# Who issues the output stores: ScalarE's queue or SyncE's, in a one-core attention and Fourier-mix kernel

## The chip, the cores and the metric

The kernel runs on one core of a Trainium2 chip. The metric is the time of one execution on the device, in microseconds (us). Eight executions of the kernel before gave a median of 308.81 us, from 307.64 to 309.92.

An engine of the core works through its own list of instructions in order: TensorE (PE) multiplies matrices, VectorE (DVE) and ScalarE (ACT) do element work, GpSimd (POOL) does some element work, and SyncE (SP) here issues transfers (DMAs) and nothing else. POOL and ACT issue DMAs too. A transfer is carried out by 16 shared DMA engines after its issue; the issuing engine goes on meanwhile. An instruction that waits holds up everything behind it on its own engine.

## The reference

Two stages, for 4 batches of 768 rows:

```python
# attention in chunks of 32 queries, each with 8 memory keys and its neighbourhood
scores = scale * np.matmul(q_c, k_full.transpose(0, 1, 3, 2))
a = softmax(scores)                      # per row
out[:, :, c_start:c_end] = np.matmul(a, v_full)
...
# x = out, heads joined: (4, 768, 512)
X = np.fft.fft(np.fft.fft(x, axis=1), axis=2)
u = x + np.real(X)
un = (u - mu) / np.sqrt(var + 1e-06)     # mean and variance of each row
ch = np.maximum(un @ w_ch1, 0.0) @ w_ch2 # 512 -> 2048 -> 512
return u + ch
```

## The kernel before, in words

**Stages.** Each batch b goes through three stages. *Attention* takes 4 pairs of heads per batch, 16 pairs n in all: POOL loads q and k (L287), SP loads v with seven DMAs of short rows (`e_load_v`, L290 to L306, into one of four tiles `va`), PE turns and multiplies, ACT takes the exponential, DVE divides (`e_norm`) into the batch's tile `xs[b]`. *Fourier*: DVE folds the rows, PE multiplies with sine and cosine tables (`ps`, L446, then `pm`, L588), DVE adds the result to the input. The upper three of a batch's six row tiles are wanted in mirrored order. For batches 1 to 3 that is done by three transfers: POOL writes the rows to DRAM (`x_rows`, L478), SP copies them there in reverse order (`x_back`, L482 and L483), POOL reads them again (`xr`, L487), and `e_sum_back` (DVE, L502 and L504) adds them to `pm`. Each DVE sum frees one of the two PSUM buffers that `pm` uses. After the sums come row statistics (L600, L601), `un` on ACT (L606) and, for batches 1 to 3, a transposing DMA on SP (`unT`, L618), which the text calls a flip. *MLP*: per half batch 16 groups of `ph` (L644) with a relu on ACT (L651), then three output tiles of 16 matmuls each (`pc`, L658). DVE makes each output tile `osb` (L664); there are three `osb` buffers.

**Outputs.** The six row tiles (0, 0 to 5) of batch 0 and tiles 0 to 2 of the later batches go straight to the output (`e_out`, L668). Tiles 3 to 5 of batches 1 to 3 lie mirrored and go in two hops: `e_out_rows` (L671) writes the tile to DRAM, and `e_out_back` (L678 and, for tile 3, L680) copies it in reverse order to the output. The MLP makes a batch's tiles in the order 0, 1, 2, 3, 4, 5 for batch 0 and 0, 3, 4, 5, 1, 2 for the others. In the text, "store (b, t)" is the transfer that takes tile t of batch b out of `osb`. In the kernel before ACT issues all 24 stores, and SP issues the second hops.

**Order.** Before anything is emitted, a planner (`Plan`, L37 to L137) runs through the tasks with guessed costs and fixes the order of every engine's list. At each step it takes, for each free engine, the first task in rank that is ready. A task is ready when its predecessors are done, and, for a task with `lag`, when they have been done for that long:

```python
if any(a["done"] is None
       or (a["end"] > now if a["engine"] == e else a["done"] > now - slack - t["lag"])
       for a in t["after"]):
```

A predecessor on the task's own engine is compared without the lag. `moved` is a guess of the transfer's time; transfers of one engine follow each other in the plan, and the task counts as done 1.4 us after that. `take` and `give` count buffers, `osb` among them. Loads of v (SP) keep their order; tasks marked `loose` may go past a load that isn't ready. The rank of a task is its place in the program, and the MLP's tasks come after all of attention and Fourier, so on SP a load of v, an `x_back` or a flip that is ready goes ahead of a second hop.

**Completion counters.** In the compiled program of the kernel before, the DMAs that SP and ACT issue take eight completion counters in turn, one common round for both engines, and a DMA waits until the previous DMA on its counter has landed, whichever engine issued that one and whatever it moved.

Of the kernel before, what the change touches and what calls it, by code (L numbers as in the profile page):

```python
# [36 lines left out]
class Plan:  # L37
# [6 lines left out]
    WARM = 14.0  # L44
    SLACK = 0.7
    FILL = 0.17
    LATER = 14.0
    filling, fill = None, None

    def __init__(self, slots):  # L50
# [3 lines left out]
    def add(self, engine, cost, emit, after=(), take=(), give=(), rank=None, moved=0.0,  # L54
            loose=False, late=0.0, filler=False, behind=None, push=False, lag=0.0):
        t = dict(engine=engine, cost=cost, emit=emit, after=[a for a in after if a is not None],
                 take=take, give=give, rank=len(self.tasks) if rank is None else rank,
                 moved=moved, done=None, at=None, no=len(self.tasks), loose=loose,
                 late=late, filler=filler, behind=behind, push=push, lag=lag)
        self.tasks.append(t)  # L60
        return t

    def order(self):
        now, idle, wire = 0.0, {}, {}
        waiting = {}
        for t in self.tasks:
            waiting.setdefault(t["engine"], []).append(t)
        for ts_ in waiting.values():
            ts_.sort(key=lambda t: (t["rank"], t["no"]))
        gives = []  # L70
        placed = []
        while any(waiting.values()):
            for tag in [g for g in gives if g[0] <= now]:
                gives.remove(tag)
                self.free[tag[1]] += 1
            moved = False
            for e, ts_ in waiting.items():
                if idle.get(e, 0.0) > now:
                    continue
                held = False  # L80
                for t in ts_:
                    slack = (self.SLACK if e == "PE" and now > self.FIRST and not t["filler"]
                             else 0.0)
                    if held and not t["loose"]:
                        continue
# [3 lines that stand above are left out]
                        held = held or (e == "SP" and not t["loose"])  # L89
                        continue  # L90
                    if t["behind"] is not None and t["behind"]["at"] is None:
                        continue
                    need = {}
                    for tag in t["take"]:
                        need[tag] = need.get(tag, 0) + 1
                    if any(self.free[tag] < m for tag, m in need.items()):
                        held = held or (e == "SP" and not t["loose"])
                        continue
                    for tag in t["take"]:
                        self.free[tag] -= 1  # L100
                    cost = t["cost"] * (2.0 if e == "PE" and now < self.WARM else 1.0)
                    idle[e] = t["end"] = now + cost
                    if t["moved"]:
                        wire[e] = max(wire.get(e, 0.0), now + cost) + t["moved"]
                        t["done"] = t["end"] = wire[e] + (2.8 if e == "POOL" else 1.4) + t["late"]
                        if t["push"] and wire.get("SP", 0.0) > now:
                            wire["SP"] += t["moved"]
                            for o in placed:
                                if o["engine"] == "SP" and o["done"] > now:
                                    o["done"] += t["moved"]  # L110
                                    o["end"] = o["done"]
                    else:
                        t["done"] = now + cost + self.LAG.get(e, 0.07)
                    for tag in t["give"]:
                        gives.append((t["done"], tag))
                    t["at"] = now
                    placed.append(t)
                    ts_.remove(t)
                    moved = True
                    break  # L120
                else:
                    if e == "PE" and self.filling and self.filling[0]["at"] is not None \
                            and self.filling[1]["at"] is None:
                        cost = self.FILL * (2.0 if now < self.WARM else 1.0)
                        idle[e] = now + cost
                        placed.append(dict(engine="PE", cost=cost, emit=self.fill, at=now,
                                           done=now + cost))
                        moved = True
            if not moved:
                times = ([v for v in idle.values() if v > now] + [g[0] for g in gives]  # L130
                         + [t["done"] + x for t in placed for x in (0.0, self.SLACK, self.LATER)
                            if t["done"] + x > now])
                assert times, [(t["engine"], t["no"], t["take"]) for ts_ in waiting.values()
                               for t in ts_[:2]]
                now = min(x for x in times if x > now)
        self.end = max(t["done"] for t in placed)
        return placed  # L137
# [3 lines left out]
def kernel(  # L141
# [11 lines left out]
    nc = tc.nc  # L153
    B, H, S, D = q.shape
    DM = out.shape[2]
    DFF = moe_w_ch1.shape[1]
    P = 128
# [35 lines left out]
    plan = Plan(dict(qs=NS, ks=NS, va=NV, kTb=NKT, qT=2, tr=1, sc=1, xa=1, e1=3,  # L193
                     xsb=3, fold=2, hl=1, up=4, dn=1, acc=2, mlp=2, un=6, unT=2, hT=1, osb=3))
# [470 lines left out]
                                       xs[b][:, st, :], ALU.mult, ALU.add)  # L665

    def e_out(b, st):
        nc.scalar.dma_start(out[b, ts(st, P), :], osb_of.pop((b, st)))  # L668

    def e_out_rows(b, st):  # L670
        nc.scalar.dma_start(od[b % 2, st - 3], osb_of.pop((b, st)))  # L671

    def e_out_back(b, st):
        t = st - 3
# [311 lines left out]
    def mlp(b, t_un, rs):  # L986
        for sh in range(2):
            relu = []
            c2 = None
            for ht in range(NHT):  # L990
                ph = add("PE", 0.65, lambda sh=sh, ht=ht: e_ch1(b, sh, ht),
                         mlp_prev + [t_un[slot(b, 3 * sh + i)] for i in range(3)] + t_w1,
                         take=(mtag(b, ht),), give=("unT",) if sh == 1 and ht == NHT - 1 else (),
                         rank=MLPS + len(plan.tasks), filler=True)
                relu.append(add("ACT", 0.5, lambda sh=sh, ht=ht: e_relu(b, sh, ht),
                                [ph, relu[-1] if relu else None],
                                take=("hT",) if ht == 0 else (), give=(mtag(b, ht),),
                                rank=RELU(len(plan.tasks))))
            for stl in range(3):
                st, end_b = slot(b, 3 * sh + stl), 3 * sh + stl == NST - 1  # L1000
                for part in range(4):
                    end = part == 3
                    c2 = add("PE", 0.88, lambda sh=sh, stl=stl, part=part: e_ch2(b, sh, stl, part),
                             [relu[4 * part + 3], t_w2[part], c2], take=(mtag(b, stl),) if part == 0 else (),
                             give=("hT",) if stl == 2 and end else (),
                             rank=MLPS + len(plan.tasks), filler=True)
                os_ = add("DVE", 0.76, lambda sh=sh, stl=stl: e_osb(b, sh, stl), [c2, rs],
                          take=("osb",), 
                          give=(mtag(b, stl), "xsb") if end_b else (mtag(b, stl),),
                          rank=RELU(len(plan.tasks)))  # L1010
                mlp_prev[0] = c2
                if b and st > 2:
                    o1 = add("ACT", 0.1, lambda st=st: e_out_rows(b, st), [os_], give=("osb",),
                             moved=0.9, late=1.5, rank=RELU(len(plan.tasks)))
                    add("SP", 0.1, lambda st=st: e_out_back(b, st), [o1], moved=2.6, loose=True,
                        lag=plan.LATER if b < B - 1 else 0.0)
                    continue
                add("ACT", 0.1, lambda st=st: e_out(b, st), [os_], give=("osb",), moved=0.9,
                    rank=RELU(len(plan.tasks)))

    def RELU(i):
        return i - MLPS
# [44 lines left out]
```

## Time and profile before

| | us |
|---|---|
| median of 8 executions | 308.81 |
| the profiled execution's own time | 309.92 |
| its span, first to last instruction | 308.2 |
| PE busy | 283.0 (92% of the span) |
| DVE busy | 168.4 (55%) |
| ACT busy | 163.0 (53%) |
| POOL busy | 45.6 (15%) |
| store issued by ACT (L668), one | 0.34 |
| first hop issued by ACT (L671), one | 0.33 |
| 256 KB second hop issued by SP (L678), one | 0.57 |
| mean granted PE clock | 0.982 of full |

In a timeline a row gives the start, the length, the engine and the line; SPq and ACTq are those engines' DMA issues, which do not count as busy. In the 40 equal slices of the page (7.7 us each) a digit is the busy share in tenths, or the granted clock in tenths of full speed. A row of the windows view gives, for a stretch, the busy time of PE, PEld (weight loads), DVE, ACT and POOL, then the granted clock, the share of the DMA engines and the GB/s.

### The profile page before, as it was taken

To read this page: it belongs to the slowest core of one execution; us is meant where nothing else is said; L and a number is where in the kernel's file an instruction comes from. 1 tells how busy PE (TensorE), PEld (TensorE's weight loads), DVE (VectorE), ACT (ScalarE), POOL (GpSimd) and SP (SyncE) were. 2 spreads that over 40 slices of the span, in tenths; PEclk is the share of its full clock that TensorE was granted. 3 is DMA by queue.
4 is the path that set the end of the run, shared out by engine and by line. 5 is a ranking of instruction groups with operands and counts; after the bars stand their busy time and mean duration, and the time that the engine had idled before them with its cause. 6 is when DMAs were issued, how large, how long until landed. Compare 5 with 4: busy or idle time off the path is not lost.

```text
span 308.2 us, 7397 instructions
## 1 busy us (share of the span) xinstructions
PE 283.0 (92%) x3086; PEld 176.5 (57%) x3086; DVE 168.4 (55%) x368; ACT 163.0 (53%) x291; POOL 45.6 (15%) x84
## 2 busy tenths in 40 slices
PE   1399998999999991799999999999999999999994
PEld 0357677866656770465578555765554554554641
DVE  7868896874298760837986949946801101002001
ACT  6656356688684762385875832572471360630710
POOL 8806421131031002111001021000010000000000
PEclk9999999999999997599999999999999999999999
DMA  6989999998487498946493225921630423103404
GB/s 117 195 174 170 208 203 197 198 200 161 88 186 152 118 140 196 176 88 178 114 169 103 53 53 188 195 97 46 130 66 34 105 34 95 43 0 89 84 34 102
DMA packets 98689, 38.36 MB, mean 124 GB/s; under 512 B 85728, under 2 KB 93920, under 8 KB 98656
## 3 DMA queue, kind: packets, MB, share of 16 engines
q1 hardware_dynamic: 84320, 16.33, 32.4%
q0 software_dynamic: 10592, 15.21, 25.2%
q10 hardware_dynamic: 3744, 6.36, 5.9%
q8 instruction: 24, 0.39, 0.5%
q14 instruction: 9, 0.07, 0.1%
HBM read 37.36 MB, written 13.37 MB: 165 GB/s over the span
## 4 chain that ended last, share of the span: by engine, by line
PE 85%; DMA 7%; POOL 2%; DVE 2%; issue 1%; SPq 1%; ACT 1%; POOLq 0%; DVEq 0%
PE pc L658 27%; PE ph L644 27%; PE xa L376 7%; PE ps L446 5%; PE idle L713 4%; PE pm L588 4%; PE ps L577 4%; PE sc L352 2%; DMA x_back<-x_rows 2%; DMA qs<-in_q_dram 2%; PE trk L314 2%; PE trq L314 2%; DMA xr<-x_back 2%; PE xo L376 1%; DVE st L600 1%
## 5 line engine op out<-in xcount | busy, mean ns | idle before, releaser
L644 PE MATMUL ph<-unT,w_sb 128*128 128x384 f16 x512 | 89.9, 329 | 0.7 <-ACT hT L651 0.6
L651 ACT ACTIVATE hT<-ph 128x384 f16<-128x384 f32 x128 | 61.0, 491 | 51.2 <-PE ph L644 49.6
L658 PE MATMUL pc<-w_sb,hT 128*128 128x512 f16 x384 | 87.5, 379 | 0.0
L644 PEld LDWEIGHTS <-w_sb 128*128 128x128 f16 x512 | 48.6, 98 | 33.9 <-issue 2.6
L664 DVE SCALAR_TENSOR_TENSOR osb<-pc,rstd,xsb 128x512 f32<-128x512 f32 x24 | 18.0, 750 | 77.1 <-PE pc L658 77.0
L658 PEld LDWEIGHTS <-hT 128*128 128x128 f16 x384 | 36.2, 98 | 41.2 <-issue 0.2
L360 ACT ACTIVATE e<-sc,mbias 128x384 f32<-128x384 f32 x64 | 33.7, 580 | 14.2 <-PE sc L352 13.5
L606 ACT ACTIVATE un<-xsb,mu_s 128x512 f16<-128x512 f32 x24 | 17.1, 718 | 23.2 <-DVE mu_s L601 23.2
L376 PE MATMUL xa<-va,e 128*64 128x65 f32 x672 | 25.7, 226 | 0.0
L376 PEld LDWEIGHTS xa<-va,e 128*64 128x64 f32 x672 | 21.9, 137 | 6.1 <-issue 4.4
L458 ACT CAST up<-ps 128x386 f16<-128x386 f32 x16 | 9.7, 604 | 14.2 <-PE ps L446 11.2
L588 PE MATMUL pm<-cosD,up 128*128 128x256 f16 x48 | 9.7, 285 | 8.2 <-DVE xsb L504 8.2
L600 DVE BATCH_NORM_STATS2 st<-xsb 128x6 f32<-128x512 f32 x24 | 16.6, 691 | 0.7
L387 DVE TENSOR_TENSOR xsb<-xa,zs 128x384 f32<-128x384 f32 x28 | 15.6, 557 | 1.0
L462 DVE TENSOR_TENSOR up<-ps,up 128x386 f16<-128x386 f32 x16 | 9.5, 596 | 11.7 <-ACT up L458 11.7
L431 ACT CAST hi<-ff 128x768 f16<-128x768 f32 x12 | 9.9, 833 | 11.5 <-DVE ff L423 11.3
L386 DVE RECIPROCAL zs<-xa 128x6 f32<-128x6 f32 x28 | 5.3, 188 | 18.9 <-PE xa L376 18.7
L323 ACT COPY qT<-trq 128x768 bf16<-128x768 bf16 x16 | 12.8, 799 | 5.2 <-PE trq L314 5.1
L588 PEld LDWEIGHTS <-up 128*128 128x128 f16 x96 | 9.3, 101 | 10.7 <-DVE xsb L504 8.6
L287 POOL DMA_DIRECT2D ks<-in_k_dram x16 | 10.4, 649 | 32.8 <-PE trk L314 30.6
L713 PE MATMUL idle<-dz 128*128 128x384 bf16 x63 | 14.0, 358 | 1.1 <-DVE zero L231 1.1
L287 POOL DMA_DIRECT2D qs<-in_q_dram x16 | 10.4, 653 | 26.4 <-PE trq L314 22.2
(137 smaller groups left out, 338.9 us busy)
## 6 DMA issues: line engine op xcount, KB each, us to landing
va<-in_v_dram SPq DMA_DIRECT2D x32, 220.0 KB
w_sb<-in_moe_w_ch_dram POOLq DMA_DIRECT2D x8, 512.0 KB, 16.9
out_dram<-osb ACTq DMA_DIRECT2D x15, 256.0 KB
qs<-in_q_dram POOLq DMA_DIRECT2D x16, 192.0 KB, 6.0
ks<-in_k_dram POOLq DMA_DIRECT2D x16, 192.0 KB, 6.2
x_rows<-xsb POOLq DMA_DIRECT2D x3, 768.0 KB, 5.0
xr<-x_back POOLq DMA_DIRECT2D x3, 768.0 KB, 5.2
out_rows<-osb ACTq DMA_DIRECT2D x9, 256.0 KB
```

The source lines that it names most:

```text
L287: nc.gpsimd.dma_start(dst[n % NS][0:QP], src[b, 2 * pr:2 * pr + 2].rearrange("h (p j) d -> p h (j d)", j=RB))
L360: nc.scalar.activation(e1[:, :, :, ts(half, 32)], sc[:, :, 0:6, ts(half, 32)], AFT.Exp, bias=mbias[:, half:half + 1], scale=1.0 / math.sqr ...
L376: nc.tensor.matmul(xa[64 * half:64 * half + 64, st, hh, 0:65], e1[:, hh, t6, :], v1[:, hh, 6 * g + t6, 0:65], start=True, stop=True)
L387: nc.vector.tensor_tensor(xs[b][:, 3 * g:3 * g + 3, 2 * pr * D:(2 * pr + 2) * D] .rearrange("p s (h d) -> p s h d", h=2), xa[:, :, :, 0:D] ...
L588: nc.tensor.matmul(pm[:, par, :], lhs, rhs[:, par, :], start=(im == 0), stop=(im == 3))
L600: nc.vector.bn_stats(st6, xs[b][:, kt, :])
L606: nc.scalar.activation(un, xs[b][:, kt, :], AFT.Identity, bias=mu_of[b][:, kt, 0:1], scale=-1.0)
L644: nc.tensor.matmul(ph[:, 0:384], w1_sb[:, dt, ts(ht, P)], unT_of[b][:, dt, sh * 384:(sh + 1) * 384], start=(dt == 0), stop=(dt == NDT - 1))
L651: nc.scalar.activation(hT_of[b, sh][:, ht, :], ph_of.pop((b, sh, ht))[:, 0:384], AFT.Relu, bias=0.0, scale=-1.0)
L658: nc.tensor.matmul(pc_of[b, sh, stl], hT_of[b, sh][:, ht, ts(stl, P)], w2_sb[:, ht, :], start=(ht == 0), stop=(ht == NHT - 1))
L664: nc.vector.scalar_tensor_tensor(osb, pc_of.pop((b, sh, stl)), rstd_of[b][:, st:st + 1], xs[b][:, st, :], ALU.mult, ALU.add)
L713: nc.tensor.matmul(fill_of[0][:, 0:384], dz, strided(dz, 0, [[0, 3], [1, P]]), start=True, stop=True)
```

## The change

The stores of batches 0 to 2 and the first hops of all batches move from ACT's list to SP's; only stores (3, 0), (3, 1) and (3, 2) stay with ACT. In the plan they are loose tasks of cost 0.5 with a lag of 4 us after the output tile, without the special early rank that they had on ACT. The second hop's lag goes from 14 to 8 us for batches 1 and 2; its predecessor is now on its own engine.

```diff
-    LATER = 14.0
...
-                         + [t["done"] + x for t in placed for x in (0.0, self.SLACK, self.LATER)
+                         + [t["done"] + x for t in placed for x in (0.0, self.SLACK, 4.0, 8.0)
...
     def e_out(b, st):
-        nc.scalar.dma_start(out[b, ts(st, P), :], osb_of.pop((b, st)))
+        (nc.scalar if b == B - 1 else nc.sync).dma_start(out[b, ts(st, P), :], osb_of.pop((b, st)))
 
     def e_out_rows(b, st):
-        nc.scalar.dma_start(od[b % 2, st - 3], osb_of.pop((b, st)))
+        nc.sync.dma_start(od[b % 2, st - 3], osb_of.pop((b, st)))
...
+                calm = b == B - 1
                 if b and st > 2:
-                    o1 = add("ACT", 0.1, lambda st=st: e_out_rows(b, st), [os_], give=("osb",),
-                             moved=0.9, late=1.5, rank=RELU(len(plan.tasks)))
-                    add("SP", 0.1, lambda st=st: e_out_back(b, st), [o1], moved=2.6, loose=True,
-                        lag=plan.LATER if b < B - 1 else 0.0)
+                    o1 = add("SP", 0.5, lambda st=st: e_out_rows(b, st), [os_], give=("osb",),
+                             moved=0.9, loose=True, lag=0.0 if calm else 4.0)
+                    add("SP", 0.5, lambda st=st: e_out_back(b, st), [o1], moved=2.6, loose=True,
+                        lag=0.0 if calm else 8.0)
                     continue
-                add("ACT", 0.1, lambda st=st: e_out(b, st), [os_], give=("osb",), moved=0.9,
-                    rank=RELU(len(plan.tasks)))
+                if calm:
+                    add("ACT", 0.1, lambda st=st: e_out(b, st), [os_], give=("osb",), moved=0.9,
+                        rank=RELU(len(plan.tasks)))
+                else:
+                    add("SP", 0.5, lambda st=st: e_out(b, st), [os_], give=("osb",), moved=0.9,
+                        loose=True, lag=4.0)
```

## The prediction

> **What bounds the kernel now.** I read the page's slices first, because PE carries 85% of the chain that ended last. PE is full nearly everywhere but in the start, and in one place in the middle:
>
> ```profile
> PE   1399998999999991799999999999999999999994
> PEclk9999999999999997599999999999999999999999
> ```
>
> The sixteenth slice (115.6 to 123.3 us) is a hole, and its clock and the next one's are low (0.7 and 0.5). The windows view, in steps of 2 us, sizes it:
>
> ```profile
> 115.00:117.00 2.00, 1.69 (x22) 0.85 (x16) 0.11 (x1) 1.91 (x4) 0.00 (x0) 1.00 0.62 108
> 117.00:119.00 2.00, 0.00 (x0) 0.00 (x0) 0.00 (x0) 0.83 (x2) 0.71 (x1) 1.00 1.06 188
> 123.00:125.00 2.00, 0.14 (x1) 0.13 (x2) 0.92 (x3) 0.00 (x0) 0.00 (x0) 0.50 1.21 222
> 125.00:127.00 2.00, 2.00 (x20) 1.23 (x18) 1.93 (x5) 0.72 (x1) 0.00 (x0) 0.50 1.36 224
> 127.00:129.00 2.00, 2.00 (x28) 1.27 (x23) 1.90 (x6) 0.72 (x1) 0.63 (x1) 0.50 1.39 175
> 129.00:131.00 2.00, 2.00 (x12) 1.06 (x10) 1.90 (x6) 1.01 (x3) 0.38 (x2) 0.80 0.58 90
> ```
>
> PE stands from 116.69 to 124.86, 8.17 us. After that its granted clock is half for some 5 us: of 0.14, 2.0, 2.0 and 2.0 busy us at 0.50, 0.50, 0.50 and 0.80 it lost 0.07 + 1.0 + 1.0 + 0.4 = 2.5 us. The hole costs 10.6 us. From 17 us to 304 us all other PE idle time is about 1.5 us (0.85 before 62, 0.58 between 174 and 200).
>
> The chain in order of time says what filled it:
>
> ```profile
> 107.51 1.79 SPq L296
> 109.34 0.31 SPq L305
> 109.75 0.57 SPq L482
> 110.36 7.38 DMA x_back<-x_rows
> 117.78 0.49 issue
> 118.29 5.63 DMA xr<-x_back
> 124.05 0.69 DVE xsb L502
> 124.86 1.89 PE pm L588 x8
> ```
>
> PE waits for the mirrored rows of batch 1. From the issue of x_back to the sum is 124.05 - 109.75 = 14.3 us, and x_back went out late, behind loads of v. What it reads was long there: POOL wrote x_rows at 85.50, and such a write takes 5.0 us to land (median of x_rows), so 90.5. The waits of SP's queue and the three timelines (SP, ACT, POOL) say why SP was late:
>
> ```profile
> SPq L296 <- DMA out_dram<-osb: 16.6, 3, 10.8
> SPq L305 <- DMA out_dram<-osb: 15.6, 1, 15.6
> ```
>
> ```profile
> 76.77 2.49 SPq L296 DMA_DIRECT2D va<-in_v_dram  x2
> 94.86 0.27 SPq L305 DMA_DIRECT2D va<-in_mem_v_dram  x1
> ```
>
> ```profile
> 89.67 0.35 ACTq L668 DMA_DIRECT2D out_dram<-osb  x1
> ```
>
> ```profile
> 85.50 0.80 POOL L478 DMA_DIRECT2D x_rows<-xsb  x1
> ```
>
> SP stood from 79.26 to 94.86 in the load of pair 9 until the first output store had landed (issued by ACT at 89.67, so 5.2 us to landing). The load has no data in common with a store: this is the common round of completion counters. The loads of pairs 10 and 11 (95.23 to 109.65) and x_back were queued behind it.
>
> **The change, part by part.**
>
> *Stores off the common round.* 21 of 24 stores leave ACT: 12 direct ones and 9 first hops. On SP a DMA now stands behind DMAs of SP alone, so the load of pair 9 no longer waits for a store that it precedes. Its last piece goes out at 79.3 instead of 94.86. Pair 10 follows at once (its va tile is free when PE has done pair 6, near 79.1); pair 11 waits for the last piece of its tile until PE has done pair 7, at 84.2. Two loads take 3.4 us each in the best rows (pair 12, 114.51 to 117.9) and 7.3 in the worst (pair 11 itself). That puts x_back between 90.5, when x_rows has landed, and 79.3 + 14.6 = 93.9. I take 91 to 94. With the 14.3 us chain the sum can start at 105 to 108.
>
> *What is late next.* In the trace DVE ends its work before that sum at 115.11, the sum takes 0.85 and PE asks at 116.69, so the sum may start at 115.84 and x_back may go out as late as 101.5 without a cost. The slack is 7 to 10 us. PE's next needs are near: the q of the turn at 127.11 was issued by POOL at 119.08, right behind xr, and moves forward with it. The hole goes whole: -10.6 us.
>
> *The stores' place on SP.* Store (0, 0) costs SP an issue. No row shows a store on SP; the nearest are 0.57 (L678, same engine, same 256 KB) and, at the other end, the 15.6 us that L305 stood. I take 0.57: on SP the stores have the higher rank number and a lag of 4 us, so x_back, ready in the plan about when ACT's store (0, 0) was, should go first. If (0, 0) and (0, 1) precede it, their tiles are ready at 89.6 and 96.6 and x_back goes at 97.2: still nothing. If (0, 2) does too (103.4), x_back goes at 104.0 and PE stands 104.0 - 101.5 = 2.5 us. At the far end, 94 + 15.6 = 109.6, the hole is back. Behind the stores on SP are loads 12 and 13, whose tiles only come free near 104.9 and 112.0, so nobody waits there.
>
> *Later batches, in times 10.6 us earlier.* x_back of batch 2 (154.0 before, with x_rows issued at 142.17) waited for load 15, which stood behind a store (139.2 to 150.05). Its sum came at 171.12 and was no wait; now it must go by 171.12 - 10.6 - 14.3 = 146.2, can go at 142.2 + 5 - 10.6 = 136.6, and stores (0, 4) and (0, 5) are ready at 137.2 and 143.4. Nothing. x_back of batch 3 can go at 190.6 - 10.6 = 180.0 and must by 214.73 - 10.6 - 14.3 = 189.8.
>
> *Second hops.* The planner tests no lag against a predecessor on the same engine, so the 8 us do nothing, and each second hop stands close behind its first, waiting for its landing: 2.0 us at the end of the trace (298.16 to 300.20), at most the 7.38 of x_back. Nine such waits are 18 to 66 us of SP. Behind them are x_back of batch 3, flips of batch 3 (before at 214 to 225; PE starts that MLP at 262.7, so 37 us of slack) and no loads. Only that x_back can pay; with two such waits ahead it goes near 186. I take nothing; the upper end is the slow rival below.
>
> *Buffers.* An osb tile is freed when its store has landed: lag 4 plus 5.2. Tiles come in threes, 3.45 us apart, with 13 us of DVE waiting before the next three. Covered.
>
> *ACT.* It loses 12 x 0.34 + 9 x 0.33 = 7.1 us of issue time and SP gains 21 x 0.57 = 12.0. PE's waits for ACT sum to 1.4 us (0.6 and 0.8), so the gain is 0 to 1.4; I take 0. The tail is the same: store (3, 2) stays on ACT.
>
> Sum: the profiled execution's 309.92 - 10.6 = 299.3; it lies 1.1 above the median of 308.81, so 298.2.
>
> *A rule against it.* The Trainium skill, "DMA: Bandwidth & Descriptors", section "Issuing engines are not separate DMA queues", says that transfers of all engines share the same 16 DMA engines and that spreading them over issuing engines saves only sequencer time. By that rule the edit trades 7.1 us of ACT for 12.0 of SP, neither on PE's path, and the time stays 308.8. The 15.6 us row speaks against leaving it at that: who issues also decides who waits.
>
> **The rivals.**
>
> *Partly hidden, about 303.* x_back goes out between 101.5 and 109.7, from store (0, 2) or a store's landing ahead of it, or a new order of PE's list opens a smaller hole elsewhere. Each us late costs one, from 300.7 (2.5 us of standing) up to 306. For it: SP issues in order, and loads of 3 us and more show a crowded queue. Against: 7 us of slack.
>
> *No change, 308.8.* The 15.6 us wait is put down by inference; if something else held the load (its tile, the DMA engines at 1.0 share), x_back stays near 109.75. Against: the load's other pieces had gone, and SP resumed 5.2 us after ACT's store.
>
> *Slower, 311.* x_back of batch 3 lands in SP's list behind first hop (1, 5). That tile is made at 210.77, so 200.2 + 0.75 in the new times; x_back goes at 201.5 and its sum starts at 215.8 instead of 204.1. PE runs out at 206.2 (its pm at 216.79 before) and gets its buffer at 216.6: 10.4 us, and 2.5 of clock, against 10.6 gained: +2.3. It decides when x_back of batch 3 goes later than 189.8. Second hops without lag speak for it; x_back's lower rank speaks against it, because it goes as soon as the plan has x_rows landed, about 20 us before that tile.
>
> **How the numbers follow.** Whole hole gone: 0.66, 296.5 to 300.5 (no cost beyond, 1.4 from ACT and some tenths below; some 2 us of new small waits above). Partly: 0.14. No change: 0.06. Slower: 0.11. Below 296.5: 0.03. 296 to 306 holds the first two and most of the last, 0.82. A measurement of this kernel tells about 0.3% from no change; faster takes the first, second and last (0.83), same 0.05, slower 0.12.
>
> **What would show it.** Right: no wait of SP's L305 or L296 for out_dram<-osb before 100 us; x_back of batch 1 issued before 97; slices without the hole and without a clock below 0.9 in the middle; pm's wait for xsb L504 gone. Wrong: an x_back behind a store in SP's timeline with PE idle 14 us later, or a new PE wait on va, osb or xr.

## The result, and the profile after

The changed kernel takes 304.75 us (median of 11 executions, 303.67 to 305.46); the kernel before, run beside it, takes 308.77 (32 executions, 306.94 to 310.29). The ratio is 0.9868, with a 95% interval of 0.9849 to 0.9887: faster by 4.0 us, or 1.3%, where 10.6 us were forecast. The profiled execution of after took 305.56, with a span of 303.9 and a mean granted PE clock of 0.997. In it each line of the kernel file has a number one lower than before (the second hop of L678 is L677 in after, and so on), because a line above them went.

The slices of PE and its clock come first, as before:

```profile
PE   1399999899999999999999999999999799999994
PEclk9999999999999999999999999999999999999998
```

The hole in the sixteenth slice is gone, and so is the low clock behind it. A shallow dip has come instead, a 7 in the thirty-second slice (235.5 to 243.1 us). SP's timeline (start, length, engine, line) shows why the hole went; the second, third and later lines follow each other directly on SP:

```profile
78.79 0.31 SPq L304 DMA_DIRECT2D va<-in_mem_v_dram  x1
...
87.14 0.31 SPq L304 DMA_DIRECT2D va<-in_mem_v_dram  x1
94.35 0.57 SPq L481 DMA_DIRECT2D x_back<-x_rows  x1
94.96 6.64 SPq L482 DMA_DIRECT2D x_back<-x_rows  x1
101.70 1.00 SPq L667 DMA_DIRECT2D out_dram<-osb  x2
```

The load of pair 9 ends at 78.79 + 0.31 = 79.1 instead of 95.1, that of pair 11 at 87.45, and x_back of batch 1 goes at 94.35 instead of 109.75, ahead of the stores. Its sum on DVE starts at 115.92 with nothing to wait for. SP's own waits now read so (total us, times, longest):

```profile
SPq L481 <- DMA x_rows<-xsb: 14.5, 3, 6.8
...
SPq L677 <- DMA out_rows<-osb: 12.0, 8, 1.7
```

No load of v waits for a store any more; x_back waits for the data that it reads, and the second hops for their first ones. From the last values of pair 7 on PE to the first `ph` of batch 2's MLP, before had 221.11 - 83.38 = 137.73 us and after has 211.42 - 84.25 = 127.17: **10.56 us less, and 10.6 were forecast**. The hole went whole. The rest of the answer lies behind it. PE has a wait that before had once, for 0.6 us:

```profile
PE ph L643 <- ACT hT L650: 4.2, 7, 0.6
```

The chain of waits shows where:

```profile
221.91 10.36 PE pc L657 x48
232.27 0.66 PE ph L643 x4
233.01 0.50 ACT hT L650
233.56 2.21 PE ph L643 x12
235.79 0.50 ACT hT L650
236.33 2.21 PE ph L643 x12
...
246.77 10.36 PE pc L657 x48
```

The second half of batch 2's MLP, 16 `ph` groups of 4 matmuls, takes 246.77 - 232.27 = 14.50 us, where before it took 10.40 (241.96 to 252.36). Every third group stops PE until ACT has made the relu of the group before it, five times. Batch 3's second half has one such stop and takes 11.29 instead of 10.40. A group needs to wait for a relu only if it writes into the PSUM buffer that the relu reads. The compiled programs say that this is so: the buffers of the 16 groups of batch 2's second half run 4 5 6 4 5 7 4 5 6 and so on before, and 4 **4** 6 4 **4** 6 4 **4** 6 4 **4** 6 4 **4** 6 5 after. In batch 3's the first pair shares: 5 **5** 6 5 4 6. The lists of PE, DVE and POOL are in the same order in both kernels, and ACT's differs by the stores alone. So it is not the order: it is the compiler's assignment of PSUM buffers, which is another one.

| span of after against before | us |
|---|---|
| last values of pair 7 on PE, 84.25 against 83.38 (PE's first `xa` matmul, 22.12 against 21.29, comes at 20.47 to 22.06 in the eleven profiles of the experiments, with the change or without it) | +0.87 |
| the hole, with its low clock | -10.56 |
| second half of the MLP of batch 2 | +4.10 |
| the same of batch 3 | +0.89 |
| other pieces, and from the last `osb` to the end (4.22 against 3.92) | +0.4 |
| sum, 303.9 - 308.2 | -4.3 |

### The profile page after: what moved, and what is told of

The parts are those of the page before. It is cut to its first block, busy times and chain, and to the rows that moved or that the text cites. A ratio compares the mean times of both kernels' runs of the same rounds, so it can differ in the third digit from the quotient of the medians.

```text
span 303.9 us, 7400 instructions
## 1 busy us (share of the span) xinstructions
PE 282.8 (93%) x3086; PEld 175.8 (58%) x3086; DVE 168.4 (55%) x368; ACT 162.9 (54%) x291; POOL 45.6 (15%) x84
## 4 chain that ended last, share of the span: by engine, by line
PE 88%; DMA 3%; POOL 2%; DVE 2%; ACT 2%; issue 1%; POOLq 0%; DVEq 0%; ACTq 0%
PE ph L643 28%; PE pc L657 27%; PE xa L375 8%; PE ps L445 5%; PE idle L712 4%; PE pm L587 4%; PE ps L576 4%; PE sc L351 3%; DMA qs<-in_q_dram 2%; PE trk L313 2%; PE trq L313 2%; ACT hT L650 1%; PE xo L375 1%; DMA out_dram<-osb 1%; DVE st L599 1%
## 5 line engine op out<-in xcount | busy, mean ns | idle before, releaser
L663 DVE SCALAR_TENSOR_TENSOR osb<-pc,rstd,xsb 128x512 f32<-128x512 f32 x24 | 18.0, 750 | 82.2 <-PE pc L657 79.3
L457 ACT CAST up<-ps 128x386 f16<-128x386 f32 x16 | 9.7, 603 | 14.3 <-PE ps L445 11.2
L386 DVE TENSOR_TENSOR xsb<-xa,zs 128x384 f32<-128x384 f32 x28 | 15.6, 558 | 1.0
L313 PE MATMUL trq<-ident_b,qs 96*64 96x96 bf16 x256 | 9.4, 222 | 5.2 <-DMA qs<-in_q_dram 5.0
L351 PE MATMUL sc<-qT,kTb 64*128 64x64 bf16 x384 | 11.5, 194 | 2.5 <-DVE kTb L340 1.7
```

The costliest lines, as they stand in the source:

```text
L313: nc.tensor.transpose(out_[64 * hh:64 * hh + 64, j * w:(j + 1) * w], src[:, hh, j * D:(j + 1) * D], eye)
L351: nc.tensor.matmul(sc[:, hh, t6, :], kT[r0:r0 + 64, t, :], qT[r0:r0 + 64, ts(t, 64)], start=True, stop=True, tile_position=(r0, 0))
L663: nc.vector.scalar_tensor_tensor(osb, pc_of.pop((b, sh, stl)), rstd_of[b][:, st:st + 1], xs[b][:, st, :], ALU.mult, ALU.add)
```

## The experiments

The theory: the edit takes out the hole (about -10 us) and the new PSUM assignment gives 5.0 us back. The rivals: the hole went only in part by the median; something else in the moved stores costs PE; or the shared buffer is a symptom of PE standing, not its cause. All kernels ran in five rounds beside the kernel before, whose median was 308.9, 309.32 and 308.46 in the three groups of runs.

### e1 and e2: the change without the sharing

In the compiled program a fourth `osb` buffer makes the sharing go. e1 has it, and nothing else, and e2 leaves the three buffers and takes the group concerned from another PSUM buffer, which the attention stage used. In the code, b is the batch, sh the half of it and ht the group of `ph`; three dots stand for lines left out:

```diff
# e1, against after (also in mkf, mkb, ident)
-        osb_of[b, st] = osb = fpool.tile([P, DM], FP32, tag="osb", bufs=3, name="osb")
+        osb_of[b, st] = osb = fpool.tile([P, DM], FP32, tag="osb", bufs=4, name="osb")
```

```diff
# e2, against after
-        ph_of[b, sh, ht] = ph = fps.tile([P, 512], FP32, tag=mtag(b, ht), name="ph")
+        if b > 1 and sh == 1 and ht % 3 == 1:
+            ph = aps.tile([P, 512], FP32, tag="xa", bufs=1, name="ph")
+        else:
+            ph = fps.tile([P, 512], FP32, tag=mtag(b, ht), name="ph")
+        ph_of[b, sh, ht] = ph
```

> The changed kernel with a fourth osb buffer in SBUF; the planner still counts three, and the order of every engine's list is that of the changed kernel. In the compiled program the PSUM buffers of ph in the second halves of the MLPs of batches 2 and 3 then take turns again, as before the change. Theory A (what ate half of the gain is that two ph groups that follow each other were given the same PSUM buffer, so PE waits for the relu between them): the stretch of 64 ph falls from 14.5 to 10.4 us and the last from 11.3 to 10.4, the time from 304.75 to about 299.7. Theory B (SP's stores themselves hold the MLP up, through transfers or late stores): no change, 304.7, and the stretch stays at 14.5.

> The changed kernel, still with three osb buffers, with every third ph group of the second halves of the MLPs of batches 2 and 3 put into a PSUM buffer that attention no longer uses. Same order of every list. Theory A (shared PSUM buffer): as with the fourth osb buffer, about 299.7, stretch 10.4 us. If instead the fourth osb buffer helped because a store frees its tile late on the chip: this one stays near 304.7.

e1: 299.68 us (298.8 to 300.72), ratio 0.9716, interval 0.9681 to 0.9751. e2: 300.37 (299.32 to 301.66), ratio 0.9734, 0.9693 to 0.9774. Both are some 5 us faster than after. The chain of e1 at the place:

```profile
221.80 10.36 PE pc L657 x48
232.16 10.40 PE ph L643 x64
242.56 10.36 PE pc L657 x48
```

The 64 matmuls are one piece again, of 10.40 us. e2 changes only where PSUM groups lie and gets the same, so the five lost us are the shared buffer's, and a lack of `osb` tiles on the chip is not needed to explain them. In after, too, DVE never waited for a store's tile before the very last one (2.8 us).

### e3 and e5: the sharing without the change

If the buffer is the cause, before must lose the same when its groups share one. e3 tried it by giving a group the tile of the group ahead:

```diff
# e3, against before
...
-        ph_of[b, sh, ht] = ph = fps.tile([P, 512], FP32, tag=mtag(b, ht), name="ph")
+        if (b, sh) == (2, 1) and ht % 3 == 1:
+            ph = pair_of[0]
+        else:
+            ph = fps.tile([P, 512], FP32, tag=mtag(b, ht), name="ph")
+            if ht % 3 == 0:
+                pair_of[0] = ph
+        ph_of[b, sh, ht] = ph
```

> The kernel before, with one edit: in the second half of the MLP of batch 2, five of the 16 ph groups (1, 4, 7, 10, 13) take the PSUM tile of the group ahead of them. All stores stay on ACT. Theory A: the stretch of 64 ph grows from 10.4 to 14.5 us, the time from 308.8 to 312.9. Theory B: no change.

e3: 308.72 us, ratio 0.9997 (0.9972 to 1.0022), and the stretch stays 10.40. This tells nothing on the theory: the program emits the second group's matmuls ahead of the first group's relu, so on one and the same tile the relu reads the later products and nothing has to wait; five groups of hidden values come from the next group's products. Two tiles in one buffer behave otherwise, since the second tile needs the first one's last reader. e5 makes them so:

```diff
# e5, against before
-        ph_of[b, sh, ht] = ph = fps.tile([P, 512], FP32, tag=mtag(b, ht), name="ph")
+        if (b, sh) == (2, 1) and ht % 3 < 2:
+            ph = aps.tile([P, 512], FP32, tag="xa", bufs=1, name="ph")
+        else:
+            ph = fps.tile([P, 512], FP32, tag=mtag(b, ht), name="ph")
+        ph_of[b, sh, ht] = ph
```

> The kernel before with one edit: in the second half of the MLP of batch 2, the 11 ph groups that are not third in their triple share one PSUM buffer that attention no longer uses, as in the compiled program of the changed kernel, where they share one of the MLP's own. All stores stay on ACT; the order of every list is that of the kernel before. Theory A (shared PSUM buffer costs PE the relu five times): the stretch of 64 ph grows from 10.4 to 14.5 us, the time from 308.9 to about 313.0. Theory B (the loss came with the stores on SP): no change, 308.9.

e5: 314.93 us (312.8 to 315.33), ratio 1.0178 (1.0134 to 1.0221). In its chain the stretch begins and ends so:

```profile
242.82 0.66 PE ph L648 x4
...
257.42 10.36 PE pc L662 x48
```

It takes 14.60 us, 4.2 more than before, with PE's waits for the relu at 3.5 us in six. The median rose by 5.6, somewhat more than that; the hole of this kernel's profiled execution was also longer, 9.1 us of standing. The price of the shared buffer is shown in both directions.

### e4 and e6: the gain from batch 0's six stores alone

Only the stores of batch 0 can stand between the load of pair 9 and x_back of batch 1. e4 moves those six to SP, e6 to POOL, both in the kernel before:

```diff
# e4, against before (in the plan: loose tasks of cost 0.5 with a lag of 4.0)
-        nc.scalar.dma_start(out[b, ts(st, P), :], osb_of.pop((b, st)))
+        (nc.scalar if b else nc.sync).dma_start(out[b, ts(st, P), :], osb_of.pop((b, st)))
```

```diff
# e6, against before (in the plan: tasks of POOL, cost 0.7)
-        nc.scalar.dma_start(out[b, ts(st, P), :], osb_of.pop((b, st)))
+        (nc.scalar if b else nc.gpsimd).dma_start(out[b, ts(st, P), :], osb_of.pop((b, st)))
```

> The kernel before with only the six stores of batch 0 issued by SP with a lag of 4 us; all others and the second hops are as before. In its compiled program no two ph groups share a buffer that did not before. If the hole of 10.6 us was made by batch 0's stores alone (the 15.6 us wait of SP): x_back of batch 1 goes out near 94, no hole, 308.8 - 10.6 = 298.2. If the stores of batches 1 and 2 on ACT matter as well (SP's waits of up to 10.8 us for them between 129 and 150): part of the gain is missing, 300 to 304.

> The kernel before with the six stores of batch 0 issued by POOL, whose DMAs use other completion counters; SP's list is unchanged and holds no store of batch 0. If SP stood for 15.6 us because its loads share a round of counters with ACT's stores: SP does not stand at pair 9, x_back of batch 1 goes out before 97, no hole, about 299.6 as with batch 0's stores on SP. If it stood for something else (the DMA engines, its tile), or if it matters that the stores lie in SP's own order: the wait and the hole stay, 308.9.

e4: 299.61 us (298.44 to 300.36), ratio 0.9711 (0.9676 to 0.9745). e6: 299.41 (298.71 to 299.94), ratio 0.9683 (0.9647 to 0.972). SP's timeline of e6, two lines that follow each other:

```profile
87.86 1.74 SPq L305 DMA_DIRECT2D va<-in_mem_v_dram  x1
93.77 0.57 SPq L482 DMA_DIRECT2D x_back<-x_rows  x1
```

x_back goes as early as in after, though here no store is in SP's list at all; in e4 it goes at 93.19. So the stores need not be in SP's order for the hole to go: it goes when no store of ACT sits in the round of counters that SP's loads use. And the other 15 stores that the change moves bring nothing: e1, with all 21 moved and no sharing, is no faster than e4 or e6.

### e7, e8 and e11: how late x_back may be

The prediction gave x_back of batch 1 a limit of 101.5 us and a price of one us per us behind it, up to the whole hole. These three start from e1 and put x_back, with the read of its result by POOL, later in the emitted order:

```diff
# e7, against e1: behind store (0, 2), which lies behind the load of pair 12
...
-        for t in plan.order():
+        todo = plan.order()
+        todo.remove(t_x2[1])
+        todo.remove(t_xr[1])
+        at = [i for i, t in enumerate(todo) if t is t_st[0, 2]][0]
+        todo[at + 1:at + 1] = [t_x2[1], t_xr[1]]
+        for t in todo:
```

```diff
# e8, against e1 (e11: the same without t_lv[12], which keeps its place)
...
+        late = [t_st[0, 2], t_x2[1], t_xr[1], t_lv[12]]
...
+        todo[at + 1:at + 1] = late
...
```

> The changed kernel with the fourth osb buffer (299.7 us), with one move in SP's list: x_back of batch 1, and its reader xr on POOL, are emitted behind store (0, 2), which lies behind the load of pair 12. Every other engine's list is the same. If the place of that x_back alone makes the hole: it goes out near 110.2 instead of 94.9, the sum starts near 124.5, PE stands 124.5 + 0.85 - 117.45 = 7.9 us and loses 2.5 of clock: 310.1. If the hole had other causes as well (the store transfers on ACT's queue, POOL's blocked loads): much of the gain stays, 300 to 305.

> The same kernel with x_back of batch 1 directly behind store (0, 2), and both ahead of the load of pair 12. Every other engine's list is the same. Store (0, 2) finds its tile at 104.15, so x_back goes out near 104.6, the sum starts at 104.6 + 14.3 = 118.9, and PE, ready at 117.45, stands 118.9 + 0.85 - 117.45 = 2.3 us. If the slack in the prediction (no cost up to 102.3 in these times) and the 14.3 us chain are right: 299.7 + 2.3 = 302.0, with the clock untouched, or up to 304.5 if so short a stand also halves the clock for 5 us. If the chain is slower in the crowded stretch: 303 to 306. If the slack is larger than thought: 299.7.

> The changed kernel with the fourth osb buffer and x_back of batch 1 directly behind store (0, 2), both ahead of the load of pair 12, which keeps its place in the program this time. Every other engine's list is the same. x_back goes out near 104.6; with a chain of 14.3 us (kernel before) to 16.0 us (the run with the late x_back) the sum starts at 118.9 to 120.6 and PE, ready at 117.45, stands 2.3 to 4.0 us: 302.0 to 303.7, and up to 2.5 more if the clock halves after so short a stand. If the slack is larger than thought: 299.7.

e7: 308.63 us (307.26 to 310.81), ratio 0.9997 (0.9964 to 1.003). SP's timeline and PE's wait:

```profile
107.06 0.57 SPq L481 DMA_DIRECT2D x_back<-x_rows  x1
```

```profile
PE pm L587 <- DVE xsb L503: 8.0, 1, 8.0
```

The hole is back, by SP's order alone, and the whole gain is gone: no store on ACT is needed for it. x_back went at 107.06, not at the expected 110.2, but its chain to the sum then took 16.0 us rather than 14.3.

e8: 314.61 us (ratio 1.0194, 1.0143 to 1.0244). The test is spoilt. With the load of pair 12 moved, that load came ahead of pair 8's multiplication by v in the program, and the two use one tile; pair 8 so reads pair 12's v (a changed computation), and PE stood 9.4 us for that load. It says nothing about x_back.

e11 is e8 mended: 304.94 us (303.86 to 307.82), ratio 0.9899 (0.9866 to 0.9931). Its SP timeline, PE's wait, and the windows from 117 us on (columns as before: PE, PEld, DVE, ACT, POOL, granted clock, DMA share, GB/s):

```profile
90.20 13.64 SPq L667 DMA_DIRECT2D out_dram<-osb  x3
103.94 0.57 SPq L481 DMA_DIRECT2D x_back<-x_rows  x1
```

```profile
PE pm L587 <- DVE xsb L503: 2.6, 1, 2.6
```

```profile
117.00:119.00 2.00, 0.00 (x0) 0.00 (x0) 0.45 (x1) 0.94 (x2) 0.00 (x0) 1.00 1.20 264
119.00:121.00 2.00, 1.64 (x18) 1.07 (x20) 1.90 (x7) 0.72 (x1) 0.00 (x0) 0.71 1.26 210
121.00:123.00 2.00, 2.00 (x30) 1.28 (x25) 1.93 (x4) 0.73 (x2) 0.63 (x1) 0.50 1.81 119
```

With the three stores ahead, x_back goes at 103.94, its sum starts 14.6 us later, at 118.55, and PE stands 2.6 us; the prediction said 104.0, 14.3 and 2.5. The clock then drops as it did behind the 8 us hole, and takes another 1.6 us (1.64 busy us at 0.71, 2.0 at 0.50, 2.0 at 0.94: 0.5 + 1.0 + 0.1). The prediction had left that out: its price of 2.5 us should have been 4.2. The median is 5.3 above e1's; the profiled execution, the second fastest of ten, has a span 3.6 above e1's, with a start 0.65 earlier, which agrees with the 4.2.

### e9 and e10: what makes the compiler share the buffer

Of what the change does, the second hop's lag and the engine of the first hops could be tried. e9 makes the lag count, by naming the output tile (on DVE) as a predecessor too; e10 leaves the first hops with ACT and moves only the direct stores:

```diff
# e9, against after (12.0 also replaces 8.0 in the planner's list of times)
-                    add("SP", 0.5, lambda st=st: e_out_back(b, st), [o1], moved=2.6, loose=True,
-                        lag=0.0 if calm else 8.0)
+                    add("SP", 0.5, lambda st=st: e_out_back(b, st), [o1] if calm else [o1, os_], moved=2.6, loose=True,
+                        lag=0.0 if calm else 12.0)
```

```diff
# e10, against after
-        nc.sync.dma_start(od[b % 2, st - 3], osb_of.pop((b, st)))
+        nc.scalar.dma_start(od[b % 2, st - 3], osb_of.pop((b, st)))
...
-                    o1 = add("SP", 0.5, lambda st=st: e_out_rows(b, st), [os_], give=("osb",),
-                             moved=0.9, loose=True, lag=0.0 if calm else 4.0)
+                    o1 = add("ACT", 0.1, lambda st=st: e_out_rows(b, st), [os_], give=("osb",),
+                             moved=0.9, late=1.5, rank=RELU(len(plan.tasks)))
```

> The changed kernel, three osb buffers, with one edit in the plan: the second hops of batches 1 and 2 also name the output tile as a predecessor, with a lag of 12 us, so that the planner keeps them 8 us behind their first hops; in the change the planner ignores the 8 us because the first hop is on SP as well. Only SP's list changes, only behind x_back of batch 3, and in the compiled program no ph groups share a buffer that did not before. Theory A with its trigger (the compiler's allocator saw the osb tiles of batch 2 held by SP, which stands at the second hops, and gave ph the buffer that was left): the stretch is 10.4 us, the time 299.7, as with four osb buffers. If the second hops play no part: 304.7.

> The changed kernel with the nine first hops given back to ACT, as before the change, and the second hops of batches 1 and 2 with the 8 us of lag, which now counts; the direct stores of batches 0 to 2 stay on SP. Theory A with its trigger: no shared ph buffer, 299.7. If SP's direct stores of batches 1 and 2 cost something by themselves: above the 299.6 of the kernel that moved batch 0's stores alone.

e9: 299.94 us (299.06 to 300.62), ratio 0.9722 (0.9686 to 0.9758). e10: 299.14 (298.3 to 300.58), ratio 0.9699 (0.9661 to 0.9737). In e10's chain the stretch is whole, as it is in e9's (231.80, 10.40):

```profile
230.84 10.40 PE ph L643 x64
```

So the sharing needs the three `osb` buffers and the second hops where the change put them: take either away and it goes (e1 changes the buffers alone, e9 the order of SP's list alone). It goes in e10 too, but e10 changes two things at once: the first hops are on ACT, and the second hops' lag counts again. No run shows whether the engine of the first hops matters by itself. In programs that were compiled and not run, putting batch 2's stores and hops back on ACT takes the sharing of batch 2's half away, and putting batch 3's first hops back does not.

**The best versions** are e10, e6, e4, e1 and e9, 299.14 to 299.94 us, all faster than both kernels and not to be told apart from each other by their intervals. e6 and e4 need the least editing.

## Why the prediction was right or wrong, point by point

- *Stores off the common round*: right. The load of pair 9 ends at 79.1 (79.3 forecast); e6 shows that POOL will do as well as SP. x_back went at 94.35, at the edge of 91 to 94, because x_rows took 8.0 us from its issue at 86.37 and not the median of 5.0 used.
- *The hole goes whole, -10.6*: right on the profiled executions, -10.56. By the medians it is smaller: e4 -9.3 and e6 -9.9. The profiled execution of before, 309.92, was the slowest of the first eight; in the three other profiles that have the hole by the same cause or by order (e3, e5, e7), PE stands 7.6, 9.1 and 8.0 us, against 8.2. Part of the missing us goes with the clock: of the 49 executions of before beside the experiments, 32 had a mean granted clock of 0.981 to 0.983, like the profiled one, and a median of 309.3, and the other 17 had 0.986 to 0.988 and 307.85. How much of the rest lies in the hole, and how much in the start, is open.
- *What is late next, and the price behind the limit*: right on the place in e11 (2.6 us for a forecast of 2.5), where the chain behind x_back took 14.6 us; in e7 it took 16.0, and PE stood 8.0 us where 107.06 - 101.5 = 5.6 follow from the limit. Too low on the price, since 2.6 us of standing cost clock as well.
- *The stores' place on SP*: right. x_back went first, and two stores took 1.00 us of issue (0.57 each taken).
- *Later batches*: right. x_back of batch 2 went at 139.08, with a limit of 146.2, and that of batch 3 at 180.91, with a limit of 189.8; PE waited for neither. The slower rival had the latter behind first hop (1, 5), which came only at 205.73, behind the first hops (1, 3) and (1, 4) at 185.69.
- ***Second hops*, "I take nothing", and *Buffers*, "Covered": here it failed.** Both hold for what stands on the chip: the second hops' waits are 12.0 us in eight, the longest 1.7, and no `osb` tile came late. But the prediction took the instructions behind the hole to keep their length, as if a new order on SP could change nothing in them. The compiled program assigned PSUM otherwise, and the term missing from the sum is 4.10 + 0.89 = 5.0 us. The rival *Partly hidden, about 303* held the outcome ("opens a smaller hole elsewhere"), by a cause that I had not named and at a chance of 0.14: PE's list is in the same order as before. That 304.75 lies between 296 and 306 is luck.
- *ACT* and the tail: ACT's lost 7.1 us of issue brought PE nothing, as taken. e4, which moves six stores, and e10, which moves twelve, come out alike. The tail cost 0.3.
- *The rule against it* (the Trainium skill, "DMA: Bandwidth & Descriptors", "Issuing engines are not separate DMA queues"): its no change is refuted by 0.9868 and 0.9683. It speaks of the engines that carry the transfers and of the time of issuing; here SP also stood 15.6 us for the landing of a store that ACT had issued.

Open: why the compiler gives neighbouring groups one buffer. It may hold the `osb` tiles of batch 2 to be in use until SP is through its second hops, so that `pc` keeps its PSUM buffer longer and `ph` is left with fewer. That fits e1, e9 and e10, but it is argued, not shown.

## What to carry to other kernels

When an engine stands for a transfer that it has no data in common with, move that transfer to another engine's list, and move only those that stand in the way: six stores gave all of the gain here. After a change to the order or the engine of transfers, look at the compiled program for which tiles got one buffer, also in engines and stages that the change doesn't touch; a wait of PE for ACT that repeats every few matmuls is its mark in the trace. A mirrored or copied tile that is needed late has a limit that can be worked out from the trace. It holds as far as the transfers behind it take the time that they took there (within 0.2 us in e11, 2.4 off in e7), and the price behind it includes the clock.

## What the runs showed of the hardware that was not expected

- A short stand of PE costs clock too. In e11 PE stood 2.6 us, and the granted clock was 0.71 and then 0.50 in the next two stretches of 2 us; after before's 8.17 us it was 0.50 for some 5 us. The Trainium skill, "TensorE: Matmul & The Clock Gate", Part 1, puts the drop behind an idle window of about 3.4 us; the measured 2.6 us was enough.
- The shared buffer costs 0.82 us per pair of groups (4.10 / 5): PE waits about 0.6 us for the 0.50 us relu, and the twelve matmuls of the next three groups take 2.21 instead of 12 x 10.40 / 64 = 1.95.
- The second piece of x_back, the single row that lies apart (L482), lasts 3.9 to 6.6 us on SP in after, where the large piece (L481) takes 0.57. Whether all of that is issue, the trace does not tell. It is no cost here, since SP has room, but it sits ahead of the stores.
